# A linear-attention and MLP kernel: DMA transposes held back behind the third x chunk, natural x loads moved to the GpSimd queue

## The chip, the cores and the metric

The kernel runs on one core of a Trainium2 chip. A time is the device time of one execution in microseconds; lower is better. TensorE (PE) multiplies matrices, VectorE (DVE), ScalarE (ACT) and GpSimd (POOL) work on elements, and SyncE (SP) does little but issue DMAs. ACT and POOL can issue DMAs too. Every DMA runs on the core's 16 DMA engines.

## What is computed

One input x of 2048 rows by 640 columns in bf16 goes through two branches, which a gate per row mixes.

```python
g = _sigmoid((x * gate_w).sum(-1, keepdims=True))
# A: linear attention, 32 heads of 20 columns
q, k, v = split(x @ wqkv)
phi = lambda t: jnp.where(t > 0, t + 1, jnp.exp(t)) + 1e-6
kv  = einsum("bhsd,bhse->bhde", phi(k), v);  z = phi(k).sum(rows)
a   = (phi(q) @ kv / (phi(q) @ z + 1e-6)) @ wo
# B: token shift mixer, then an MLP of 1728 columns
h  = _gelu(_layernorm(x) @ w1)
x1 = x + shift(h) @ w2
b  = x1 + _gelu(_layernorm(x1) @ w3) @ w4
out = g * a + (1 - g) * b
```

(The block is shortened: `split`, `shift` and `phi(k).sum(rows)` stand for several lines each.)

## The kernel before

The 2048 rows are 16 chunks of 128. x is needed in SBUF in two forms. In the natural form, `x_sb` (a part of the buffer RXH), a chunk's rows lie on the partitions; in the turned form, `xT` (the buffer RXT), its columns do. TensorE contracts over partitions, so the products with the weights read `xT`, and the products that sum over rows (`g_step`, line 264) read `x_sb`.

Chunks 0 to 2 are loaded in natural form and turned by TensorE: `x_tr` (lines 317 to 323) makes five 128x128 transposes into two PSUM buffers, VectorE copies three of the results to `xT` (line 322) and ACT two (line 323). Chunks 3 to 15 are turned on the way in, by DMA transposes on the SP queue (`load_xT`, line 155), in nine pieces of one to three chunks, and are loaded in natural form a second time (`load_x`, line 152), in five pieces. `late_loads` (line 280) issues both kinds on SP in an alternating order, and behind them the weights wq, w1, wv, wo and w2. The first transpose is held back by a small trick: VectorE writes one column of chunk 3 of `xT` with a memset (line 328), and since the transpose overwrites that column it must wait for the memset. The other transposes stand behind it in SP's queue.

The instruction order on each engine is the order of the program (`manual_schedule`). DMAs share eight completion semaphores in turn, so each also waits for the DMA eight places earlier to have landed.

The first stage computes k = x @ wk for one chunk after another. `k_mm(c, p, dc)` (lines 253 to 256) is one pair of matmuls: row block dc of five of the weights, 512 and 130 columns, into PSUM buffer p. The weights arrive in four DMAs: row blocks 0, 1 and 2 on the ACT queue (line 162) and blocks 3 and 4 together on SP (line 169). For chunks 0 to 2 the pairs are taken in an order by hand (lines 325 to 343), so that TensorE has work while weights and chunks arrive. From chunk 3 on the loop at line 346 does five pairs per chunk, and after them `k_post` (ACT's exp at line 247, VectorE's lines 250 and 251, which read PSUM and release its buffer). From chunk 5 on the loop also interleaves `g_unit`, matmuls of line 264 on `x_sb` of chunks two or three places back. There are four PSUM buffers, passed round by `alloc` and `release`.

The second stage (line 388) computes q with wq, the later ones (lines 421 to 637) the mixer, the MLP and the gated sum. VectorE and ACT read `x_sb` for the layer norm (lines 218 and 229), chunk 3 first at the tenth chunk of the k stage.

Of the kernel before, what the change touches and what calls it, by code (L numbers as in the profile page):

```python
# [16 lines left out]
def kernel(  # L17
# [13 lines left out]
    nc = tc.nc  # L31
    P = 128
# [29 lines left out]
    xT = RXT[:].rearrange("p (j s) -> p j s", j=DC)  # L62
# [7 lines left out]
    x_sb = RXH[:, 0:NCH * D].rearrange("p (c d) -> p c d", c=NCH)  # L70
# [78 lines left out]
    xv = x2.rearrange("(c p) d -> p c d", p=P)  # L149

    def load_x(c0, c1):
        sp.dma_start(x_sb[:, c0:c1, :], xv[:, c0:c1, :])

    def load_xT(c0, c1):
        sp.dma_start_transpose(xT[:, :, c0 * P:c1 * P], x2[c0 * P:c1 * P, :])
# [97 lines left out]
    def k_mm(c, p, dc):  # L253
        for (n0, n1) in ((0, 512), (512, KW)):
            mm(PP[p][:, n0:n1], lhsT=xT[:, dc, c * P:(c + 1) * P], rhs=wkg[:, dc, n0:n1],  # L255
               start=(dc == 0), stop=(dc == DC - 1))
# [21 lines left out]
            g_post(i, gp[0])  # L278

    def late_loads():  # L280
        load_xT(3, 4)
        load_xT(4, 5)
        load_x(3, 4)
        load_xT(5, 6)
        load_xT(6, 7)
        load_x(4, 6)
        load_xT(7, 8)
        load_xT(8, 10)
        load_x(6, 9)
        load_xT(10, 11)  # L290
        load_xT(11, 13)
        load_x(9, 12)
        load_xT(13, 16)
        load_x(12, 16)
        rows = lambda w, a, b: w[:, a:b].rearrange("(j p) d -> p j d", p=P)
        sp.dma_start(wq, rows(A_wqkv, 0, D))
        sp.dma_start(w1, rows(B_w1, 0, D))
        sp.dma_start(wv, rows(A_wqkv, 2 * D, 3 * D))
        sp.dma_start(wo6[0:GW, 0:5, :], A_wo[0:5 * GW, :].rearrange("(g r) d -> r g d", r=GW))
        sp.dma_start(wo6[0:gsz[5], 5, :], A_wo[5 * GW:D, :])  # L300
        sp.dma_start(w2[:, 0:4, :], B_w2.rearrange("(g c) d -> c g d", c=CG)[0:P])
        for g in range(4):
            sp.dma_start(w2[32 * g:32 * (g + 1), 4, :], B_w2[CG * g + P:CG * (g + 1), :])
        w1g = w1.rearrange("p k (g c) -> p k g c", c=CG)
        w1x4 = w1x.rearrange("p k (g c) -> p k g c", g=4)
        for g in range(4):
            nc.gpsimd.tensor_copy(w1x4[:, :, g, :], w1g[:, :, g, P:CG])
# [9 lines left out]
    def x_tr(c, a, b):  # L317
        ta, tb = PP[a][:, 0:512].bitcast(BF16), PP[b][:, 0:512].bitcast(BF16)
        for dc in range(DC):
            t, k = (ta, dc) if dc < 3 else (tb, dc - 3)  # L320
            nc.tensor.transpose(t[:, k * P:(k + 1) * P], x_sb[:, c, dc * P:(dc + 1) * P], ident[:])
        nc.vector.tensor_copy(xT[:, 0:3, c * P:(c + 1) * P], ta[:, 0:3 * P].rearrange("p (j s) -> p j s", j=3))  # L322
        act(xT[:, 3:5, c * P:(c + 1) * P], tb[:, 0:2 * P].rearrange("p (j s) -> p j s", j=2), ACT.Copy)
# [1 line left out]
    for _ in range(3):  # L325
        alloc()
    x_tr(0, 3, 2)
    nc.vector.memset(xT[:, 0, 3 * P:3 * P + 1], 0.0)
    late_loads()
    x_tr(1, 1, 2)  # L330
    k_mm(0, 0, 0)
    k_mm(1, 1, 0)
    k_mm(0, 0, 1)
    k_mm(1, 1, 1)
    x_tr(2, 3, 2)
    k_mm(2, 2, 0)
    k_mm(2, 2, 1)
    for c in range(3):
# [348 lines left out]
```

## Time and profile before

| what | value |
|---|---|
| median of 3 runs | 266.31 us (266.26 to 266.87) |
| profiled execution | 267.08 us, of which the span from first to last instruction is 265.4 us |
| granted TensorE clock | 1.000 |
| DMA traffic | 23.95 MB in 42207 packets, 31052 of them under 512 B |
| issue time of a DMA transpose on SP | 1.2 to 2.8 us, median 1.27 us |
| landing of a DMA transpose | 3.0 to 5.2 us after issue, median 4.0 us |
| landing of a natural x load | 3.5 to 5.2 us after issue, median 4.7 us |

The page gives the busy time of each engine and its share of the span, then the span in 40 equal slices of 6.6 us with the busy share in tenths. The chain of waits is followed back from the last instruction, at each step to whatever released it. A timeline line has the start and the length in microseconds, engine, line, operation, destination and source, a count, and in brackets the idle time before it with what ended it. "SPq" means that the SP queue is issuing a DMA. A line of a DMA queue gives packets, megabytes and the time its packets took as a share of the 16 engines; packets in flight overlap, so this can pass 100%.

### The profile page before, as it was taken

To read this page: it belongs to the slowest core of one execution; us is meant where nothing else is said; L and a number is where in the kernel's file an instruction comes from. 1 tells how busy PE (TensorE), PEld (TensorE's weight loads), DVE (VectorE), ACT (ScalarE), POOL (GpSimd) and SP (SyncE) were. 2 spreads that over 40 slices of the span, in tenths; PEclk is the share of its full clock that TensorE was granted. 3 is DMA by queue.
4 is the path that set the end of the run, shared out by engine and by line. 5 is a ranking of instruction groups with operands and counts; after the bars stand their busy time and mean duration, and the time that the engine had idled before them with its cause. 6 is when DMAs were issued, how large, how long until landed. Compare 5 with 4: busy or idle time off the path is not lost.

```text
span 265.4 us, 4180 instructions
## 1 busy us (share of the span) xinstructions
PE 259.8 (98%) x1666; PEld 134.8 (51%) x1666; DVE 127.2 (48%) x227; ACT 109.7 (41%) x163; POOL 35.5 (13%) x118
## 2 busy tenths in 40 slices
PE   6999999999999999999999999999999999999995
PEld 2555555555564445554444455555544444555552
DVE  2386659888995257999920044233200002233242
ACT  3466654555454771334977512022034444022020
POOL 7000043030200000446870000000000000000000
PEclk9999999999999999999999999999999999999999
DMA  6899994452252069992542001001000000001001
GB/s 197 162 207 236 367 252 95 99 52 49 50 57 44 11 160 385 340 137 49 108 94 49 0 2 49 25 27 49 27 25 0 0 2 0 25 27 49 25 27 49
DMA packets 42207, 23.95 MB, mean 90 GB/s; under 512 B 31052, under 2 KB 41420, under 8 KB 42188
## 3 DMA queue, kind: packets, MB, share of 16 engines
q1 hardware_dynamic: 41602, 23.16, 36.4%
q10 hardware_dynamic: 586, 0.53, 0.6%
q8 instruction: 13, 0.21, 0.3%
q14 instruction: 6, 0.05, 0.1%
HBM read 12.86 MB, written 3.44 MB: 61 GB/s over the span
## 4 chain that ended last, share of the span: by engine, by line
PE 96%; DMA 2%; DVE 0%; ACTq 0%; ACT 0%; issue 0%
PE pp L637 20%; PE pp L570 20%; PE pp L421 8%; PE pp L596 8%; PE pp L555 8%; PE pp L264 8%; PE pp L255 8%; PE pp L388 8%; DMA RA<-in_A_wqkv_dram 2%; PE pp L579 2%; PE pp L622 1%; PE pp L631 1%; PE pp L586 1%; PE pp L455 1%; PE pp L441 1%; PE pp L468 0%
## 5 line engine op out<-in xcount | busy, mean ns | idle before, releaser
L637 PE MATMUL pp<-RB,RXH 128*128 128x512 bf16 (+1 forms) x390 | 54.4, 299 | 0.0
L570 PE MATMUL pp<-lnxT,RA 128*128 128x512 bf16 x240 | 52.1, 379 | 0.0
L637 PEld LDWEIGHTS <-RXH 128*128 128x128 bf16 x390 | 29.6, 98 | 24.2 <-issue 2.1
L570 PEld LDWEIGHTS <-RA 128*128 128x128 bf16 x240 | 23.4, 98 | 28.1
L599 ACT ACTIVATE RXH<-pp,g_all 128x640 f32<-128x640 f32 x16 | 12.7, 794 | 54.9 <-PE pp L596 54.9
L572 ACT ACTIVATE RXH<-pp 128x1024 bf16<-128x1024 f32 x24 | 24.3, 1020 | 26.7 <-PE pp L570 26.7
L247 ACT ACTIVATE eb<-pp 128x640 bf16<-128x640 f32 (+1 forms) x26 | 21.4, 828 | 25.0 <-PE pp L388 16.1
L264 PE MATMUL pp<-RPK,RXH 128*128 128x512 bf16 (+1 forms) x160 | 25.2, 299 | 0.0
L255 PE MATMUL pp<-RA,RXT 128*128 128x512 bf16 (+1 forms) x160 | 24.1, 299 | 1.0 <-DMA RA<-in_A_wqkv_dram 0.5
L601 DVE SCALAR_TENSOR_TENSOR RPK<-RPK,omg,RXH 128x640 f32<-128x640 f32 x8 | 7.1, 885 | 36.5 <-ACT RXH L599 36.5
L388 PE MATMUL pp<-RXT,RA 128*128 128x512 bf16 x100 | 23.2, 379 | 0.0
L596 PE MATMUL pp<-Mp,pqT 128*128 128x512 bf16 (+1 forms) x160 | 23.1, 299 | 0.0
L555 PE MATMUL pp<-w,RXH 128*128 128x512 bf16 (+1 forms) x160 | 21.9, 299 | 0.0
L601 DVE SCALAR_TENSOR_TENSOR RXT<-RXT,omg,RXH 128x640 f32<-128x640 f32 x8 | 7.1, 885 | 24.6 <-ACT RXH L599 24.6
L421 PE MATMUL pp<-lnxT,RB 128*128 128x512 bf16 x80 | 18.3, 380 | 0.0
L264 PEld LDWEIGHTS <-RXH 128*128 128x128 bf16 x160 | 12.7, 98 | 10.4
L255 PEld LDWEIGHTS <-RXT 128*128 128x128 bf16 x160 | 12.4, 98 | 10.8 <-DVE RXT L322 0.9
L596 PEld LDWEIGHTS <-pqT 128*128 128x128 bf16 x160 | 12.2, 98 | 10.0 <-issue 0.8
L555 PEld LDWEIGHTS <-RXH 128*128 128x128 bf16 x160 | 12.3, 98 | 9.6
L606 DVE SCALAR_TENSOR_TENSOR RXH<-pp,omg,RXT 128x640 bf16<-128x640 f32 x8 | 7.1, 884 | 19.8 <-PE pp L637 19.8
L606 DVE SCALAR_TENSOR_TENSOR RXH<-pp,omg,RPK 128x640 bf16<-128x640 f32 (+2 forms) x9 | 7.3, 810 | 19.1 <-PE pp L637 17.2
L388 PEld LDWEIGHTS <-RA 128*128 128x128 bf16 x100 | 11.1, 117 | 9.1
(107 smaller groups left out, 251.4 us busy)
## 6 DMA issues: line engine op xcount, KB each, us to landing
out_dram<-RXH SPq DMA_DIRECT2D x15, 160.0 KB, 1.8
RA<-in_B_w_dram SPq DMA_DIRECT2D x5, 432.0 KB, 6.7
RA<-in_A_wqkv_dram SPq DMA_DIRECT2D x2, 800.0 KB, 6.8
RB<-in_B_w_dram SPq DMA_DIRECT2D x1, 1120.0 KB
RXH<-in_A_x_dram SPq DMA_DIRECT2D x2, 480.0 KB, 5.1
RB<-in_B_w_dram SPq DMA_DIRECT2D x1, 960.0 KB, 12.2
RB<-in_B_w_dram SPq DMA_DIRECT2D x1, 800.0 KB, 8.5
Mp<-Mscr SPq DMA_DIRECT2D x1, 800.0 KB
```

Source lines behind the costliest of these rows:

```text
L247: act(e[:, 0:n], src, ACT.Exp)
L255: mm(PP[p][:, n0:n1], lhsT=xT[:, dc, c * P:(c + 1) * P], rhs=wkg[:, dc, n0:n1], start=(dc == 0), stop=(dc == DC - 1))
L264: mm(PP[p][:, n0:n1], lhsT=x_sb[:, c, i * P:(i + 1) * P], rhs=pk[:, c, n0:n1], start=(c == 0), stop=(c == NCH - 1))
L388: mm(PP[p][:, tt * 512:(tt + 1) * 512], lhsT=wqp[:, dc, j], rhs=xT[:, dc, t0:t0 + 512], start=(dc == 0), stop=(dc == DC - 1))
L421: mm(PP[p][:, tt * 512:(tt + 1) * 512], lhsT=lh, rhs=lnxT[:, dc, t0:t0 + 512], start=(dc == 0), stop=(dc == DC - 1))
L555: mm(PP[p][:, n0:n1], lhsT=hsT[:, fc, 2 + c * P:2 + (c + 1) * P], rhs=w2[:, fc, n0:n1], start=(fc == 0), stop=(fc == DC - 1))
L570: mm(PP[p][:, k * 512:(k + 1) * 512], lhsT=w3[:, dc, (fc + k) * P:(fc + k + 1) * P], rhs=lnxT[:, dc, t * 512:(t + 1) * 512], start=(dc == ...
L572: act(h2T[:, t % 2, fc:fc + 2, :], PP[p][:].rearrange("p (k s) -> p k s", k=2), ACT.Gelu_apprx_tanh)
L596: mm(PP[p][:, n0:n1], lhsT=pqT[:, j, c * P:(c + 1) * P], rhs=Mp[:, j, n0:n1], start=(j == 0), stop=(j == DC - 1))
L601: nc.vector.scalar_tensor_tensor(x1(c), x1(c), omg[:, c:c + 1], ga, op0=ALU.mult, op1=ALU.add)
L606: nc.vector.scalar_tensor_tensor(oc[:, n0:n1], PP[p][:, n0:n1], omg[:, c:c + 1], x1(c)[:, n0:n1], op0=ALU.mult, op1=ALU.add)
L637: mm(PP[p][:, n0:n1], lhsT=h2T[:, k, fc, cc], rhs=w4[:, fc, n0:n1], start=False, stop=(fc == NF - 1))
```

## The change

In `late_loads` all nine transposes now come first on the SP queue, and the five natural loads are issued by GpSimd. The call of `late_loads` moves behind `x_tr(2, 3, 2)`, and `x_tr(2, 3, 2)` itself moves up, ahead of the pairs of weight row block 1. The memset that holds the transposes stands behind the copies of chunk 2, and a second memset, on one column of chunk 3 of `x_sb`, holds the natural loads in the same way.

```diff
     def late_loads():
-        load_xT(3, 4)
-        load_xT(4, 5)
-        load_x(3, 4)
-        load_xT(5, 6)
-        load_xT(6, 7)
-        load_x(4, 6)
-        load_xT(7, 8)
-        load_xT(8, 10)
-        load_x(6, 9)
-        load_xT(10, 11)
-        load_xT(11, 13)
-        load_x(9, 12)
-        load_xT(13, 16)
-        load_x(12, 16)
+        for (c0, c1) in ((3, 4), (4, 5), (5, 6), (6, 7), (7, 8), (8, 10), (10, 11), (11, 13), (13, 16)):
+            load_xT(c0, c1)
+        for (c0, c1) in ((3, 4), (4, 6), (6, 9), (9, 12), (12, 16)):
+            nc.gpsimd.dma_start(x_sb[:, c0:c1, :], xv[:, c0:c1, :])
         rows = lambda w, a, b: w[:, a:b].rearrange("(j p) d -> p j d", p=P)
...
     x_tr(0, 3, 2)
-    nc.vector.memset(xT[:, 0, 3 * P:3 * P + 1], 0.0)
-    late_loads()
     x_tr(1, 1, 2)
     k_mm(0, 0, 0)
     k_mm(1, 1, 0)
+    x_tr(2, 3, 2)
+    nc.vector.memset(xT[:, 0, 3 * P:3 * P + 1], 0.0)
+    nc.vector.memset(x_sb[:, 3, 0:1], 0.0)
+    late_loads()
     k_mm(0, 0, 1)
     k_mm(1, 1, 1)
-    x_tr(2, 3, 2)
     k_mm(2, 2, 0)
```

## What was predicted

> **What bounds the kernel now.** I read first the page's engine line and slices, then the chain of waits over the first 20 us, then the timelines of TensorE and of the SP queue, then the DMA view cut to windows. TensorE holds the span:
>
> ```profile
> PE 259.8 (98%) x1666; PEld 134.8 (51%) x1666; DVE 127.2 (48%) x227; ACT 109.7 (41%) x163; POOL 35.5 (13%) x118
> PE   6999999999999999999999999999999999999995
> DMA  6899994452252069992542001001000000001001
> PE 96%; DMA 2%; DVE 0%; ACTq 0%; ACT 0%; issue 0%
> ```
>
> TensorE is idle for 5.6 of 265.4 us, and only in the first and the last slices. The DMA row beside it is full in the first slices: while chunks of x arrive the 16 engines are busy. The chain and the timeline say where the early idle time lies:
>
> ```profile
> 1.79 4.86 DMA RA<-in_A_wqkv_dram
> 7.40 0.29 PE pp L321 x5
> 7.71 0.39 ACT RXT L323
> 8.15 7.25 PE pp L255 x52
> ...
> 5.23 0.91 PE L255 MATMUL pp<-RA,RXT 128*128 128x512 bf16 x4
> 6.69 0.70 PE L255 MATMUL pp<-RA,RXT 128*128 128x512 bf16 x4 [0.55 <-DMA RA<-in_A_wqkv_dram]
> 7.23 0.44 PE L321 MATMUL pp<-ident,RXH 128*128 128x128 bf16 x5
> 8.15 7.25 PE L255 MATMUL pp<-RA,RXT 128*128 128x512 bf16 x52 [0.47 <-ACT RXT L323]
> ```
>
> TensorE waits 0.55 us for the second row block of the K weights (landed 6.65), turns x chunk 2 from 7.23, and waits 0.47 us for the copies of it. From 8.15 on it never stops until the last outputs, so a microsecond won or lost before 8.15, and any new wait after it, reaches the end one for one. The SP queue in this stretch issues without a pause:
>
> ```profile
> 4.97 2.60 SPq L155 DMA_TRANSPOSE RXT<-in_A_x_dram  x2
> 7.62 0.58 SPq L152 DMA_DIRECT2D RXH<-in_A_x_dram  x1
> 8.24 2.53 SPq L155 DMA_TRANSPOSE RXT<-in_A_x_dram  x2
> 10.82 0.58 SPq L152 DMA_DIRECT2D RXH<-in_A_x_dram  x1
> 11.44 2.58 SPq L155 DMA_TRANSPOSE RXT<-in_A_x_dram  x2
> ```
>
> A transpose of one chunk takes SP about 1.27 us. Those issued at 8.24 and 9.46 landed after 3.4 and 3.0 us. The natural loads stand between the transposes in the same queue: that order throttles them.
>
> **What the Trainium skill says.** "DMA: Bandwidth & Descriptors", section "Issuing engines are not separate DMA queues": DMAs of SP, ACT and GpSimd run on the same 16 engines and interleave; issuing from more engines saves issue time alone. Section "Queues, rings and completion order": an engine goes round its queues packet by packet. The trace agrees for two queues of equal packets; from 3 to 6 us SP's and ACT's loads moved almost equal numbers:
>
> ```profile
> q1 hardware_dynamic: 425, 0.50, 54.3%
> q10 hardware_dynamic: 388, 0.45, 41.5%
> ```
>
> It shows no transpose beside a load of another queue. In "SWDGE vs HWDGE vs iDMA" the page says that GpSimd DMAs have their descriptors written by software, with the first byte after about 1 us; no run here shows it yet. "SBUF — State Buffer" (the "DVE blocks DMA" trap) adds that this writing and VectorE's 2-port modes exclude each other; the trace of before has no such DMA.
>
> **The change, part by part.**
>
> Order of TensorE. The 5 transposes of chunk 2 move from after k_mm(1, 1, 1) to before k_mm(0, 0, 1). Chunk 2 of x is issued at 1.7 and lands after 4.7 us (the longest of the L152 landings there), so at 6.4. TensorE turns it at 6.45 to 6.9 instead of standing still for 0.55 us. The four matmuls of row block 1 (0.54 us, 6.69 to 7.23) follow to 7.45; VectorE's copy (0.36 after a 0.37 us lag, 7.18) and ACT's (0.38 us) are done by then, so the 0.47 us wait goes. What stood at 8.15 begins at about 7.49. Gain 0.66 us. Next late would be weight rows 3 and 4 (issued 2.18, landing 5.6, so 7.8), needed only after five more pairs of 0.273 us, at 8.9: hidden.
>
> The hold. The first transpose waits for a VectorE memset that now follows the copy of chunk 2: copy at 6.82, memset at about 7.2, issue at 7.25 instead of 4.97, 2.3 us later. Queued behind it on SP are all nine transposes and then the weights wq, w1, wv, wo, w2; on VectorE nothing waits behind 0.06 us memsets (its next work is the exp of chunk 0 near 10). The weights lose nothing: taking five loads out of the queue gives back 4 x 0.58 + 1.5 = 3.8 us of SP. What the hold buys I put at zero, between 0 and 0.3: the transposes' small packets begin only near 6.2 by the traffic rate, when the weight block that TensorE waited for had all but arrived.
>
> Transposes alone. With a cadence of 1.27 us and 3.2 us to landing, chunks 3 to 7 land at 10.45, 11.7, 13.0, 14.3, 15.5. TensorE wanted them at 11.15 (8.15 plus 11 pairs of 0.273), 12.5, 13.9, 15.94, 17.98 by the chain; less 0.66 that is 10.5, 11.85, 13.2, 15.3, 17.3. All are in time, the first three by 0.05 to 0.2 us. The margin of over 2 us that chunk 3 had is spent.
>
> Natural loads on POOL. Five DMAs, 13 chunks, start behind the second memset at about 7.3 with POOL idle until 33, so the first bytes move at about 8.3 (skill's 1 us), the rest about one DMA per us. Nobody needs them soon: chunk 3 is first read by L264 at 17.4. But now nothing throttles them. Prices from windows where one kind runs alone (23.2 to 24.8 us transposes, 26 to 31 us loads):
>
> ```profile
> q1 hardware_dynamic: 1685, 0.43, 127.3%
> ...
> q1 hardware_dynamic: 1492, 1.87, 106.1%
> ```
>
> A 256 B packet costs 1.273 x 16 x 1.6 / 1685 = 19 ns of an engine, a 1,280 B row 1.061 x 16 x 5 / 1492 = 57 ns. A transposed chunk is 640 small packets, 40 an engine, 0.77 us; a natural chunk is 8 rows an engine, 0.455 us, all 13 together 5.9 us. Transposes use 0.77 of each 1.27 us, so 0.5 us per slot is free. The question is how an engine shares:
> - transposes favoured (they go as several small packets against one row): no stall, 0 to 0.3 us;
> - in order of arrival: before chunk 5 stand 6 natural chunks, 2.73 us, less three free slots of 0.5: 1.2 us late, 14.2 against 13.2; before chunk 7 all 13, 5.9 less 2.5: 3.4 us late, 18.9 against 17.3. Stall 1.6 us;
> - one row for each small packet: chunk 3 meets 8 rows, chunks 4 and 5 forty each, 88 x 57 ns = 5.0 us less 1.5: chunk 5 lands at 16.5 against 13.2. Stall 3.3 us.
> The sharing seen above (near equal packets) speaks for the last, the GpSimd's slower supply for the second. I take the middle, 2.5 us. The stall falls in TensorE, with no slack behind.
>
> Sum: -0.66 + 2.5 = +1.8 us on the profiled run, 267.08 us (span 265.4 and 1.7 around it); that run lies 0.77 us above the median of 266.31, and the difference carries over: 268.1 us.
>
> **Rivals.**
> - Forecast: the natural loads crowd the transposes; 267.3 (arrival order) to 269.0 (one for one). For it: DMA slices at 0.8 to 1.0 while both are being loaded. Against: rows and small packets never met across queues in this trace.
> - Not slower: transposes keep their pace, and the reorder's 0.66 us remains less 0 to 0.3: 265.65 to 266.0. It decides as long as a transposed chunk needs no more than about 1.3 us in the engines, that is if fewer than 9 rows (0.5 us) get ahead of its 40 packets. For it: such packets may be handed over in larger groups. This is a no-change by measurement.
> - Lock: descriptor writing on POOL and VectorE's L250 (324 ns, bf16) hold each other up near 10 to 13 us. VectorE frees PSUM for TensorE with little to spare (L251 of chunk 0 ends at 12.28, chunk 4 starts at 12.5), so a block of about 1 us costs 0.8: 266.4 to 267.4, with the transposes otherwise in time. POOL may be done by then, which speaks against it.
> - More gained than I count: weight block 1 and chunk 2 land some 0.3 us sooner without small packets about, 265.3. Against it: they overlap by a few tenths at most.
>
> **How the numbers follow.** Forecast 0.50, transposes keep pace 0.33, lock 0.10, larger gain 0.07. About 0.3%, 0.8 us, is what a measurement of this kernel can tell from no change. Slower by more: 0.46 of the forecast case and 0.08 of the others, 0.54. Faster by more needs under 265.5: the larger gain and a sliver of the second case, 0.12. The rest, 0.34, is within. The range 265.6 to 269.2 takes the second case at its favourable end and the one-for-one sharing at the other; the forecast's own is 267.2 to 269.1.
>
> **What would show it.** Right: L321 in one run of ten to fifteen before the second weight block, no 0.47 us wait on L323, the first transpose at about 7.25, then TensorE waiting for DMA RXT<-in_A_x_dram around chunks 4 to 7, 1.6 to 3.3 us in all, while a GpSimd queue fills the DMA row. Wrong: no such wait and transposes landing in 3 us as before; or waits on VectorE for PSUM instead; or transposes with long landings whose chunks TensorE still has.

## The result and the profile after

| kernel | median of its runs | range | ratio to before (95% interval) |
|---|---|---|---|
| before | 266.36 us (6 runs) | 266.26 to 266.87 | |
| changed | 277.97 us (6 runs) | 275.74 to 278.50 | 1.0421 [1.0384, 1.0459] |

The change costs 11.6 us where 1.8 were forecast, and the time lies above the range, which ended at 269.2. The profiled execution took 278.5 us, with a span of 276.8, so the span grew by 11.4 us. Here and in the table of experiments a ratio leaves out runs more than 1.5% above the fastest of the same kernel, which now and then occur whatever the kernel; e2_pool keeps one run of four that way and has no ratio.

The page of the changed kernel: busy time by engine, then the slices (6.9 us each), then the two queues that issue most DMAs.

```profile
PE 261.1 (94%) x1634; PEld 136.2 (49%) x1666; DVE 127.6 (46%) x228; ACT 109.8 (40%) x163; POOL 39.2 (14%) x123
PE   7725999999999999999999999999999999999995
PEclk9995999999999999999999999999999999999999
DMA  5799995145043205999254100010010000001001
q1 hardware_dynamic: 39858, 21.03, 32.6%
q0 software_dynamic: 496, 2.13, 3.4%
```

Two things are new. TensorE's row has a hole in the third slice (13.8 to 20.8 us), and the granted clock has a dent in the fourth, right behind it. From the fifth slice on both rows are as before: the whole loss lies before 28 us. The second queue, q0, is GpSimd's: 2.13 MB in 496 packets. 416 of these carry the data, which is 5,120 B or four rows of x each, where the queues of SP and ACT move one row of 1,280 B a packet.

The timeline of the changed kernel from 4 to 30 us (start, length, engine, what, and in brackets the idle time before it):

```profile
6.99 3.84 PE L255 MATMUL pp<-RA,RXT 128*128 128x512 bf16 x25
7.43 21.99 SPq L155 DMA_TRANSPOSE RXT<-in_A_x_dram  x9
7.74 3.82 POOL L284 DMA_DIRECT2D RXH<-in_A_x_dram  x5 [1.43 <-DVE RXH L323]
11.07 1.52 PE L255 MATMUL pp<-RA,RXT 128*128 128x512 bf16 x10 [0.25 <-DVE eb L250]
14.57 1.54 PE L255 MATMUL pp<-RA,RXT 128*128 128x512 bf16 x10 [1.98 <-DVE eb L250]
23.62 2.86 PE L255 MATMUL pp<-RA,RXT 128*128 128x512 bf16 x10 [7.51 <-DMA RXT<-in_A_x_dram]
26.27 1.27 PE L264 MATMUL pp<-RPK,RXH 128*128 128x512 bf16 x4
```

The groups of ten are chunks 3, 4 and 5. Before them TensorE stands for 0.25, 1.98 and 7.51 us, 9.74 in all. The first two waits are put down to VectorE's L250, but these matmuls do not read `eb`: the transpose of chunk 3 landed at 10.93, and that of chunk 4, issued at 8.77, landed 5.8 us later, at 14.53. The transposes issued at 10.08 and 11.4 landed after 13.5 and 12.8 us; before the change the slowest of this stretch took 4.0. SP issued one after the other with gaps of 0.05 us, so none of them stood waiting for one of the shared semaphores. The chain of waits of the changed kernel says it in three pieces (start, length, what):

```profile
8.77 1.26 SPq L155
10.03 0.04 issue
10.08 13.50 DMA RXT<-in_A_x_dram
...
23.62 2.86 PE pp L255 x10
26.48 1.07 PE pp L264 x4
```

Chunk 5 then takes 2.86 us instead of about 1.4, and the four L264 matmuls 1.07 instead of 0.54. The view by windows shows why (window, length, busy time and count of PE, PEld, DVE, ACT and POOL, granted clock, DMA share, GB/s):

```profile
14.00:16.00 2.00, 1.43 (x10) 0.73 (x10) 1.36 (x3) 0.00 (x0) 0.00 (x0) 1.00 1.04 314
16.00:20.00 4.00, 0.11 (x2) 0.00 (x0) 1.15 (x2) 1.48 (x4) 0.00 (x0) 1.00 1.28 115
20.00:25.00 5.00, 1.38 (x5) 0.65 (x6) 0.00 (x0) 0.00 (x0) 0.00 (x0) 0.58 1.05 183
25.00:30.00 5.00, 4.95 (x28) 2.66 (x28) 1.39 (x3) 1.74 (x5) 0.00 (x0) 0.74 1.15 157
...
21.00:27.50 6.50, 3.88 (x15) 1.93 (x16) 0.25 (x1) 0.77 (x2) 0.00 (x0) 0.50 1.29 183
```

After the long idle the clock is granted at half: 0.50 from 21 to 27.5 us (0.58 and 0.74 are means over windows that hold some time at full rate). The Trainium skill, "TensorE: Matmul & The Clock Gate", section "Why this matters for your kernels", says that an idle gap of more than about 3 us drops TensorE to half rate. The trace agrees: the gap of 1.98 us left the clock at 1.00, the one of 7.51 us did not (the 2.44 us wait of e10_held_paced, below, puts the bound lower). The same rows show the DMA engines counted as full throughout, but from 14 to 16 us they deliver 314 GB/s, and after that only 115 and 183.

The sum: idle 9.7 us, chunk 5 slow by 1.5, L264 by 0.5, less 0.4 us that TensorE was ahead before chunk 3 (its earlier pairs end at 10.83 here; the same 11 pairs, 22 matmuls, counted from 8.15 in the kernel before end at 11.2). That is 11.3 of the 11.4 us by which the span grew.

### The profile page after: what moved, and what is told of

Its sections match the earlier page's. It is cut to its first block, busy times and chain, and to the rows that moved or that the text cites. A ratio compares the mean times of both kernels' runs of the same rounds, so it can differ in the third digit from the quotient of the medians.

```text
span 276.8 us, 4156 instructions
## 1 busy us (share of the span) xinstructions
PE 261.1 (94%) x1634; PEld 136.2 (49%) x1666; DVE 127.6 (46%) x228; ACT 109.8 (40%) x163; POOL 39.2 (14%) x123
## 3 DMA queue, kind: packets, MB, share of 16 engines
q0 software_dynamic: 496, 2.13, 3.4%
## 4 chain that ended last, share of the span: by engine, by line
PE 91%; DMA 5%; SPq 1%; issue 1%; DVE 1%; ACT 0%
PE pp L628 19%; PE pp L561 19%; PE pp L264 8%; PE pp L412 8%; PE pp L587 8%; PE pp L546 8%; PE pp L379 8%; PE pp L255 6%; DMA RXT<-in_A_x_dram 5%; PE pp L570 2%; PE pp L613 1%; PE pp L622 1%; PE pp L301 1%; SPq L155 1%; PE pp L577 1%
## 5 line engine op out<-in xcount | busy, mean ns | idle before, releaser
L628 PE MATMUL pp<-RB,RXH 128*128 128x128 bf16 (+1 forms) x382 | 53.9, 298 | 0.4
L561 PEld LDWEIGHTS <-RA 128*128 128x128 bf16 x240 | 23.4, 98 | 28.0
L247 ACT ACTIVATE eb<-pp 128x640 bf16<-128x640 f32 (+1 forms) x26 | 21.4, 828 | 37.0 <-PE pp L255 20.8
L255 PE MATMUL pp<-RA,RXT 128*128 128x130 bf16 (+1 forms) x156 | 26.2, 314 | 9.9 <-DMA RXT<-in_A_x_dram 7.5
L264 PE MATMUL pp<-RPK,RXH 128*128 128x512 bf16 (+1 forms) x158 | 25.6, 302 | 0.1
L255 PEld LDWEIGHTS <-RXT 128*128 128x128 bf16 x160 | 13.1, 103 | 20.6 <-DMA RXT<-in_A_x_dram 10.2
L546 PE MATMUL pp<-w,RXH 128*128 128x128 bf16 (+1 forms) x157 | 21.7, 297 | 0.2
L250 DVE TENSOR_SCALAR eb<-eb 128x640 bf16<-128x640 bf16 (+1 forms) x26 | 9.6, 371 | 22.8 <-ACT eb L247 22.8
L264 PEld LDWEIGHTS <-RXH 128*128 128x128 bf16 x160 | 12.9, 99 | 10.8 <-issue 0.6
```

The costliest lines, as they stand in the source:

```text
L247: act(e[:, 0:n], src, ACT.Exp)
L264: mm(PP[p][:, n0:n1], lhsT=x_sb[:, c, i * P:(i + 1) * P], rhs=pk[:, c, n0:n1], start=(c == 0), stop=(c == NCH - 1))
L546: mm(PP[p][:, n0:n1], lhsT=hsT[:, fc, 2 + c * P:2 + (c + 1) * P], rhs=w2[:, fc, n0:n1], start=(fc == 0), stop=(fc == DC - 1))
L561: mm(PP[p][:, k * 512:(k + 1) * 512], lhsT=w3[:, dc, (fc + k) * P:(fc + k + 1) * P], rhs=lnxT[:, dc, t * 512:(t + 1) * 512], start=(dc == ...
L628: mm(PP[p][:, n0:n1], lhsT=h2T[:, k, fc, cc], rhs=w4[:, fc, n0:n1], start=False, stop=(fc == NF - 1))
```

## The experiments

All were compared with the kernel before on the same chip, whose medians lay between 266.5 and 266.9 us.

| run | what is different | median, us | ratio (95% interval) |
|---|---|---|---|
| e1_hold | changed, loads all on SP in the old order | 267.61 | 1.0031 [1.0007, 1.0055] |
| e2_pool | before, natural loads on GpSimd | 276.81 | none |
| e3_reorder | before, chunk 2 turned earlier | 266.40 | 0.9991 [0.9975, 1.0007] |
| e4_act | changed, ACT in GpSimd's place | 276.30 | 1.0345 [1.0310, 1.0381] |
| e5_pool2 | before, 3 chunks on GpSimd | 266.74 | 1.0004 [0.9982, 1.0026] |
| e6_act2 | before, the same 3 on ACT | 267.05 | 1.0009 [0.9994, 1.0024] |
| e7_serial | changed, transposes after the loads | 278.52 | 1.0451 [1.0428, 1.0475] |
| e8_half | changed, loads in half columns | 273.82 | 1.0296 [1.0255, 1.0337] |
| e9_paced | before, 13 chunks on GpSimd, paced | 266.95 | 1.0017 [0.9997, 1.0037] |
| e10_held_paced | changed, paced | 270.76 | 1.0143 [1.0107, 1.0179] |
| e11_pool6 | before, 6 chunks on GpSimd at once | 273.12 | 1.0210 [1.0163, 1.0257] |
| e12_early_paced | e9_paced, chunk 2 turned earlier | 266.18 | 0.9998 [0.9985, 1.0012] |
| e13_act6 | before, 6 chunks on ACT, a little later | 269.33 | 1.0110 [1.0054, 1.0166] |
| e14_pool6 | the same on GpSimd | 268.43 | 1.0050 [0.9992, 1.0108] |
| e15_extra_act | before, 0.88 MB extra on ACT | 268.26 | 1.0046 [1.0021, 1.0070] |
| e16_extra_pool | the same on GpSimd | 267.76 | 1.0043 [1.0028, 1.0058] |
| e17_other_src | changed, natural loads from B_x | 277.15 | 1.0387 [1.0337, 1.0438] |
| e18_plain256 | changed, plain loads for transposes | 268.94 | 1.0089 [1.0056, 1.0122] |

### Which part of the change costs the time

e1_hold keeps the hold and the early turning of chunk 2 and puts the old list of `late_loads` back, all on SP:

```diff
-        for (c0, c1) in ((3, 4), (4, 5), (5, 6), (6, 7), (7, 8), (8, 10), (10, 11), (11, 13), (13, 16)):
-            load_xT(c0, c1)
-        for (c0, c1) in ((3, 4), (4, 6), (6, 9), (9, 12), (12, 16)):
-            nc.gpsimd.dma_start(x_sb[:, c0:c1, :], xv[:, c0:c1, :])
+        load_xT(3, 4)
+        load_xT(4, 5)
+        load_x(3, 4)
...
```

> Only the hold and the earlier turning of chunk 2; all loads stay on the SP queue in the alternating order of the kernel before. Theory A (a second queue of natural loads beside the transposes makes them crawl, whichever engine issues it) and theory B (only loads issued by GpSimd do, for their 5,120 B packets): 265.8 us, between 265.4 and 266.4, every transpose landing within 4 us. Theory C (holding the transposes for 2.3 us is what makes them late): 268 us or more, with TensorE waiting for transposes of chunks 3 to 5.

Measured: 267.61 us, between what the theories said. The hold spends the margin, and with it comes a wait. Timeline of e1_hold:

```profile
6.15 6.52 PE L255 MATMUL pp<-RA,RXT 128*128 128x512 bf16 x45
13.85 1.54 PE L255 MATMUL pp<-RA,RXT 128*128 128x512 bf16 x10 [1.18 <-DMA RXT<-in_A_x_dram]
18.48 1.54 PE L255 MATMUL pp<-RA,RXT 128*128 128x512 bf16 x9 [0.64 <-DMA RXT<-in_A_x_dram]
```

The transposes of chunks 5 to 9 landed after 3.3 to 5.3 us (3.0 to 4.0 before), but the first was issued 1.7 us later (6.65 in place of 4.97), and TensorE stood 1.8 us. Hold and early turn together cost about 0.8 us (0.3%), a fraction of the loss.

e2_pool is the other part alone: nothing held, chunk 2 at its old place, natural loads on GpSimd.

```diff
     def late_loads():
-        load_xT(3, 4)
-        load_xT(4, 5)
-        load_x(3, 4)
-        ...
+        for (c0, c1) in ((3, 4), (4, 5), (5, 6), (6, 7), (7, 8), (8, 10), (10, 11), (11, 13), (13, 16)):
+            load_xT(c0, c1)
+        for (c0, c1) in ((3, 4), (4, 6), (6, 9), (9, 12), (12, 16)):
+            nc.gpsimd.dma_start(x_sb[:, c0:c1, :], xv[:, c0:c1, :])
...
     nc.vector.memset(xT[:, 0, 3 * P:3 * P + 1], 0.0)
+    nc.vector.memset(x_sb[:, 3, 0:1], 0.0)
     late_loads()
```

> Only the natural loads on GpSimd; nothing is held, chunk 2 is turned where it was. A and B: the transposes that meet the natural loads crawl as in the changed kernel, one of chunks 4 to 6 landing over 8 us after its issue; 272 to 278 us. C: 266.3 us, as before.

Measured: 276.81 us (270.43 to 279.37 in four runs); all four lie above the 268.91 us of the slowest of 33 runs of the kernel before, but the spread is wide, so the size of the loss is not settled by this run. In the profile, which is of the slowest run, the transposes issued at 7.6 and 8.9 us landed after 13.4 and 17.7 us, and TensorE waited 7.13 and 2.21 us for them. The long landings come with GpSimd's loads, held or not.

e3_reorder moves only `x_tr(2, 3, 2)` ahead of the second pair of weights:

```diff
     k_mm(1, 1, 0)
+    x_tr(2, 3, 2)
     k_mm(0, 0, 1)
     k_mm(1, 1, 1)
-    x_tr(2, 3, 2)
```

> Only the transposes of chunk 2 on TensorE ahead of weight block 1; transposes start at about 5 us as before. All theories: 265.7 us (between 265.4 and 266.1), the 0.47 us wait on ACT's copy of chunk 2 gone. If the change gains nothing here either, the gain I counted at 0.66 us is not there.

Measured: 0.9991 [0.9975, 1.0007], nothing that can be told. In its profile TensorE waited 0.89 us for chunk 2 of x, which landed at 6.9, in place of 0.55 us for the weights. Turning chunk 2 earlier exchanges one wait for another, and which is longer depends on whichever transfer happens to land last.

### GpSimd, or any second queue? And how much?

e4_act is the changed kernel with the five loads on ACT's queue:

```diff
+        for (c0, c1) in ((3, 4), (4, 6), (6, 9), (9, 12), (12, 16)):
+            aq.dma_start(x_sb[:, c0:c1, :], xv[:, c0:c1, :])
...
-        for (c0, c1) in ((3, 4), (4, 6), (6, 9), (9, 12), (12, 16)):
-            nc.gpsimd.dma_start(x_sb[:, c0:c1, :], xv[:, c0:c1, :])
```

> The changed kernel with the natural loads issued by ACT instead of GpSimd, so a second queue with packets of one 1,280 B row. A: transposes crawl as with GpSimd or worse, 274 to 285 us. B: transposes land within 5 us, TensorE waits at most 2 us for them, 265.7 to 268.5 us.

Measured: 276.30 us, but for another reason. Timeline of e4_act, and under it what held ACT up (engine, line, what it waited for, us):

```profile
6.68 9.96 ACTq L282 DMA_DIRECT2D RXH<-in_A_x_dram  x5
11.75 1.52 PE L255 MATMUL pp<-RA,RXT 128*128 128x512 bf16 x10 [1.81 <-DMA RXT<-in_A_x_dram]
18.77 4.31 PE L255 MATMUL pp<-RA,RXT 128*128 128x512 bf16 x20 [5.50 <-DVE RPK L251]
...
ACT eb L247 <- DMA RXT<-in_A_x_dram: 10.0, 1, 10.0
```

From its first issue to its last ACT took 9.96 us, where GpSimd took 3.82 for the same five DMAs. An issue alone takes ACT 0.33 to 0.50 us. The rest is waiting for completion semaphores: the fourth load was issued at 9.31, when ACT's own first had landed (9.29), and the fifth at 16.26, when the transpose of chunk 5 had landed (16.24). SP and ACT take turns with the same eight semaphores; in the changed kernel each of GpSimd's five loads has one of its own and waits for none. So ACT's exp came late, PSUM stayed occupied and TensorE waited for VectorE. The transposes landed after 4.8 to 6.9 us, 6.9 for chunk 5. Its landing at 16.2 is close to the 16.5 us of the prediction's one-for-one sharing, but does not show that sharing: from 6.7 to 16.3 us 2894 small packets went through beside 1152 rows. The total time says nothing about the queue here.

The next runs vary the amount, at first three chunks on either queue:

```diff
     def late_loads():
+        for (c0, c1) in ((3, 4), (4, 6)):
+            nc.gpsimd.dma_start(x_sb[:, c0:c1, :], xv[:, c0:c1, :])
         load_xT(3, 4)
         load_xT(4, 5)
-        load_x(3, 4)
...
-        load_x(4, 6)
```

> Order and start of the transposes as before; only the first two natural loads (chunks 3 to 5, 6 of the 26 packets an engine gets from GpSimd in the changed kernel) go to GpSimd, the other three stay between the transposes on SP. Theory B (loads issued by GpSimd slow the transposes beyond their own traffic): chunk 4 or 5 lands over 5 us after its issue, 267.5 to 270.5 us. Theory A (any second queue, one packet for one, nothing beyond the traffic): chunk 5 at most 2 us late, which its margin covers, 266.0 to 267.0 us.

> The same two loads on ACT's queue instead of GpSimd's, everything else as in e5_pool2. A: like e5_pool2 within 0.5 us. B: no transpose lands later than 5 us after its issue and the time stays at 266.0 to 267.2 us, while e5_pool2 is slower.

Measured: 1.0004 and 1.0009, both no change; transposes landed after 3.8 to 5.7 and 3.9 to 5.8 us. Three chunks do no harm that can be told, whoever issues them. e11_pool6 adds (6, 9) to the list on GpSimd.

> As e5_pool2, with a third load on GpSimd at once (chunks 3 to 8, 12 of 26 packets an engine). E: the backlog is twice that of e5_pool2 and falls on chunks 5 to 7, whose margin is 2 us; one of them lands 5 to 9 us after issue, 266.5 to 271 us, between e5_pool2 and the kernel with all five. If the crawl needs the largest loads only: as e5_pool2, 266.0 to 267.0 us.

Measured: 273.12 us. The transpose issued at 7.6 landed after 10.8 us, those behind it after 9.9, 9.2 and 9.1, and TensorE stood 5.15 us and then ran chunk 5 in 2.85. With 0, 3, 6 and 13 chunks handed to GpSimd at once the times are 266.5, 266.7, 273.1 and, in the changed kernel, 278.0 (276.8 in e2_pool): issued this early, the harm begins between three and six.

### Are the loads slow by themselves, or do both kinds disturb each other?

e7_serial lets no transpose run beside the loads: GpSimd copies a column of the last natural chunk into `xT`, which the first transpose must wait for.

```diff
         for (c0, c1) in ((3, 4), (4, 6), (6, 9), (9, 12), (12, 16)):
             nc.gpsimd.dma_start(x_sb[:, c0:c1, :], xv[:, c0:c1, :])
+        nc.gpsimd.tensor_copy(xT[:, 0, 3 * P:3 * P + 1], x_sb[:, 15, 0:1])
+        for (c0, c1) in ((3, 4), (4, 5), (5, 6), (6, 7), (7, 8), (8, 10), (10, 11), (11, 13), (13, 16)):
+            load_xT(c0, c1)
```

> The changed kernel with the first transpose held until the last natural load of GpSimd has landed, so the two kinds never meet. B: alone, the loads need about 7 us (landed by 15), the transposes then land at 1.3 us intervals from 18 on; TensorE waits once, about 7 us, and warms up again: 272 to 276 us, less than the changed kernel although everything that TensorE needs starts 8 us later. Rival D (GpSimd's loads are slow by themselves, with or without transposes beside them): the loads end at 20 or later, and the time is 280 us or more.

Measured: 278.52 us, later than expected. Timeline of e7_serial:

```profile
7.72 3.83 POOL L282 DMA_DIRECT2D RXH<-in_A_x_dram  x5 [1.41 <-DVE RXH L324]
17.66 0.18 POOL L283 COPY RXT<-RXH 128x1 bf16<-128x1 bf16 x1 [6.11 <-DMA RXH<-in_A_x_dram]
17.87 13.12 SPq L155 DMA_TRANSPOSE RXT<-in_A_x_dram  x9
20.89 5.93 PE L255 MATMUL pp<-RA,RXT 128*128 128x512 bf16 x30 [10.04 <-DMA RXT<-in_A_x_dram]
```

Alone, the loads landed 2.6 to 6.8 us after issue (beside the transposes 3.0 to 12.8) and all were there before 17.7. Then the transposes took 2.9 us each, at a cadence of 1.3, which puts chunk 5 at 23.4. In the changed kernel it landed at 23.57. So running both kinds together brought chunk 5 no sooner than running them one after the other. The DMA view over one and the same window, 7.4 to 23.6 us, shows what the overlap was worth (queue: packets, MB, share of 16 engines). The changed kernel:

```profile
q0 software_dynamic: 496, 2.13, 58.9%
q1 hardware_dynamic: 2907, 0.71, 38.9%
```

and e7_serial:

```profile
q0 software_dynamic: 496, 2.13, 40.9%
q1 hardware_dynamic: 2189, 0.54, 15.5%
```

The window is 16.2 us, or 259 us of 16 engines. The same 2.13 MB took 0.589 x 16.2 = 9.5 us of each engine beside transposes and 6.6 us alone. A small packet took 0.389 x 259 / 2907 = 35 ns beside loads and 18 ns alone, which is the 19 ns of the prediction. The mixture takes 98% of the window for what would cost 58% at the prices of either kind alone (2907 x 19 ns and 1664 rows x 57 ns are 150 of 259 us). These are times in flight, which overlap (the windows of the prediction's prices reach 106 and 127%), so they are no measure of a limit; the landings above show the loss without them.

The 35 ns are an average that hides how the loss comes about. Of the 2907 small packets (256 B, and some of 4 B), 2641 took 22 ns or less, as they do alone; 192 took over 100 ns, up to 819, and about half of the time is theirs. GpSimd's packets have a median of 225 ns, with single ones up to 3361. More than half of these long packets fall between 16 and 22 us, where the traffic drops to 125 GB/s, from 216 between 7.4 and 16.

e8_half cuts each load in two halves of the columns. Of its 576 data packets 416 are of 4,480 B (seven pieces of 640 B), the rest smaller; the changed kernel's are of 5,120.

```diff
-            nc.gpsimd.dma_start(x_sb[:, c0:c1, :], xv[:, c0:c1, :])
+            for (h0, h1) in ((0, D // 2), (D // 2, D)):
+                nc.gpsimd.dma_start(x_sb[:, c0:c1, h0:h1], xv[:, c0:c1, h0:h1])
```

> The changed kernel with each natural load cut into two of half the columns, rows of 640 B. If GpSimd's packets are four rows (5,120 B in the changed kernel), they become 2,560 B and twice as many. If the cost goes with the number of changes between the two kinds on an engine: slower than the changed kernel, 280 us or more. If it goes with the size of the packet that each small one waits for: faster, 270 to 276 us.

Measured: 273.82 us, with waits of 0.96, 0.25, 1.47, 1.40 and 2.08 us spread over the chunks and none long enough for the clock. But GpSimd also needed 7.26 us to issue ten DMAs where it needed 3.82 for five, so the loads arrived more slowly: the run loses less than the changed kernel, and does not tell packet size from pace.

### Pace

e9_paced hands GpSimd three chunks at once and the other ten one at a time, each held by a memset on VectorE behind a `k_post`; nothing else is held.

```diff
+    def pool_x(c):
+        if 6 <= c < NCH:
+            nc.vector.memset(x_sb[:, c, 0:1], 0.0)
+            nc.gpsimd.dma_start(x_sb[:, c, :], xv[:, c, :])
...
+            for (c0, c1) in ((3, 4), (4, 6)):
+                nc.gpsimd.dma_start(x_sb[:, c0:c1, :], xv[:, c0:c1, :])
...
         k_post(c, p)
+        pool_x(c + 5)
```

(Four GpSimd copies that wait for w1 also move behind the loop, since they would stand ahead of the loads.)

> All 13 natural chunks on GpSimd as in the changed kernel, nothing held, chunk 2 turned where it was; but only chunks 3 to 5 at once, chunks 6 to 15 one at a time, each behind a memset after the k stage's element work of five chunks earlier. Theory E (it is the backlog that GpSimd's queue builds up beside the transposes, not the queue or the bytes): transposes land within 5 us, no wait of TensorE for them, 266.0 to 267.0 us. Theory B (GpSimd's loads slow transposes whatever their pace): 270 us or more.

Measured: 266.95 us, 1.0017 [0.9997, 1.0037]. All 13 chunks go through GpSimd's queue and the loss is gone: the transposes landed after 3.9 to 7.4 us, where 5 had been expected, but TensorE never waited for one. e10_held_paced is the changed kernel with the same pacing.

> The changed kernel itself, with hold and early turning of chunk 2, but its natural loads paced as in e9_paced. E: the hold alone is left, at most 1 us of waits for chunks 3 to 5 against about 0.4 us gained at the start: 265.9 to 267.2 us. B: 270 us or more.

Measured: 270.76 us, above what was expected. Timeline of e10_held_paced:

```profile
10.17 1.52 PE L255 MATMUL pp<-RA,RXT 128*128 128x512 bf16 x10 [0.38 <-DMA RXT<-in_A_x_dram]
12.34 2.90 PE L255 MATMUL pp<-RA,RXT 128*128 128x512 bf16 x20 [0.65 <-DMA RXT<-in_A_x_dram]
21.77 2.86 PE L255 MATMUL pp<-RA,RXT 128*128 128x512 bf16 x10 [2.44 <-DMA RXT<-in_A_x_dram]
```

Later transposes landed after up to 9.4 us, somewhat more than in e9_paced, and the hold has used up the margin that covered the delay there. The chunk after the 2.44 us wait again takes 2.86 us, and the clock from 21.4 to 24.7 us is granted at 0.50. e12_early_paced is e9_paced with chunk 2 turned earlier, as in e3_reorder, and no hold.

> e9_paced with chunk 2 turned early and the transposes not held: the version that should keep the gain at the start and nothing else. E: 265.7 to 266.5 us, at best 0.5 us under the kernel before, which these rounds may not tell from no change. B: 270 us or more.

Measured: 266.18 us over 22 runs, 0.9998 [0.9985, 1.0012]. Its profile still shows one wait of 0.89 us for a late transpose. No version beat the kernel before by an amount that can be told.

### The twins: queue and packet size

e13_act6 and e14_pool6 differ in one word of the program. The transposes of chunks 3 and 4 go out as before; three loads (six chunks) go to the second queue behind the turning of chunk 2.

```diff
     x_tr(2, 3, 2)
+    nc.vector.memset(x_sb[:, 3, 0:1], 0.0)
+    for (c0, c1) in ((3, 4), (4, 6), (6, 9)):
+        aq.dma_start(x_sb[:, c0:c1, :], xv[:, c0:c1, :])
+    late_loads()
```

> x chunks 3 to 8 in natural form issued at once (three DMAs) on ACT's queue behind x_tr(2) at its old place, the rest of late_loads on SP, nothing held, chunk 2 turned at its old place. The same six chunks on GpSimd in e11_pool6 gave 273.1 us and transposes that landed 9 to 11 us after issue. Theory G (it is the issue by GpSimd as such, with its large packets or without): transposes land at most 6.5 us after issue, TensorE waits for RXT under 1 us in all, 266.0 to 268.5 us. Theory Q (any second queue with so much waiting data does it): transposes land 8 us or more after issue, 269 to 274 us. ACT's own standing at the issue may hold its exp and copies; that is read apart, by the landings.

> The twin of e13_act6, line for line, with GpSimd issuing the three loads in place of ACT. Both theories: transposes issued beside the loads land 8 us or more after issue, TensorE waits 3 us or more for RXT, 269 to 274 us. If this one keeps its transposes under 6.5 us, then the place of the issue decided in e11_pool6 and not the amount.

Measured: 1.0110 [1.0054, 1.0166] on ACT and 1.0050 [0.9992, 1.0108] on GpSimd; the intervals overlap, and neither expectation was met. Transposes landed after 5.9 to 7.2 us beside ACT's loads and 2.9 to 8.9 beside GpSimd's, with medians of 6.4 and 6.6. In the profiles TensorE waited 1.0 us for transposes on GpSimd and none on ACT, where weights that landed late (1.1 us) had set it back anyway. So a second queue delays the transposes whoever issues it. The DMA view from 8 to 16 us of e13_act6,

```profile
q1 hardware_dynamic: 2878, 0.70, 51.0%
q10 hardware_dynamic: 686, 0.83, 50.0%
```

and of e14_pool6:

```profile
q0 software_dynamic: 206, 0.87, 56.5%
q1 hardware_dynamic: 1915, 0.47, 35.5%
```

For equal load data (0.83 and 0.87 MB) 2878 small packets went through beside ACT's loads and 1915 beside GpSimd's, one profile each. The twins are not quite alike in time: ACT's second and third loads waited for landed transposes, by the shared semaphores, and the third was issued at 10.58, GpSimd's at 9.74. Both mixtures are dear: at the prices of either kind alone (19 and 57 ns) ACT's is worth 94 of the 129 us that it took and GpSimd's 75 of 118, factors of 1.4 and 1.6, where the changed kernel's 150 of 253 are 1.7. That e11_pool6, with the same six chunks on GpSimd 1.8 us earlier, lost 2% shows how near the edge this amount lies.

e15_extra_act and e16_extra_pool keep every load of the kernel before and add two loads with rows of 3,456 B behind the turning of chunk 2.

```diff
+    nc.vector.memset(lnxT[:, 0, 0:1], 0.0)
+    for dc in range(2):
+        aq.dma_start(lnxT[:, dc, 0:F], B_w3[dc * P:(dc + 1) * P, :])
```

> The loads of the kernel before, in its order on SP, and behind x_tr(2) two extra loads on ACT's queue of 128 rows of 3,456 B each (0.88 MB in all) that move data nobody uses into a buffer that is free then. It is about as much data as six x chunks (0.98 MB), with rows 2.7 times as long. Theory F (large packets hold the transposes up, whoever issued them): transposes beside them land 7 us or more after issue and the time is 269 us or more. Theory G (the issue by GpSimd as such): transposes land at most 6.5 us after issue, 266.0 to 268.5 us.

> The twin of e15_extra_act with the two extra loads (data nobody uses) on GpSimd. Theories F and G both: transposes beside them land 7 us or more after issue, 269 us or more. If the transposes of this one land under 6.5 us, the delay belongs to many rows of x on GpSimd and not to GpSimd's loads in general.

Measured: 1.0046 and 1.0043, transposes landing after 2.8 to 5.4 and 4.7 to 6.2 us, and no wait for one in either profile; where their 0.4% come from is not shown. Neither long rows nor GpSimd as the issuer is enough by itself. In these two the transposes stay spaced by plain loads in SP's own queue, which the six-chunk twins lack.

### Where the data come from, and what kind of small packet

e17_other_src changes only the source of GpSimd's loads:

```diff
-            nc.gpsimd.dma_start(x_sb[:, c0:c1, :], xv[:, c0:c1, :])
+            nc.gpsimd.dma_start(x_sb[:, c0:c1, :], xbv[:, c0:c1, :])
```

> The changed kernel, with GpSimd's five natural loads reading the same rows of B_x, an input of the same shape that the reference never uses, in place of A_x; x in natural form is therefore not x for chunks 3 to 15. Number, size and order of all DMAs stay. Theory S (transposes and natural loads delay each other because both read the same tensor in DRAM): transposes land at most 7 us after issue, TensorE waits under 2 us for RXT, 266.5 to 270 us. Theory Q (13 chunks waiting on GpSimd's queue at once hold the transposes up, wherever they come from): chunk 5 lands 12 us or more after issue, 275 to 279 us, as the changed kernel (277.97).

Measured: 277.15 us, and chunk 5 landed 11.7 us after issue, a hair under the 12 expected. Up to that landing, at 21.3, its small packets took 28 ns on average, so the loss does not hang on one fixed price. That both kinds read one tensor is not the cause.

e18_plain256 replaces the transposes by plain loads of the same 256 B pieces:

```diff
-        sp.dma_start_transpose(xT[:, :, c0 * P:c1 * P], x2[c0 * P:c1 * P, :])
+        for c in range(c0, c1):
+            sp.dma_start(xT[:, :, c * P:(c + 1) * P], x2[c * P:(c + 1) * P, :].rearrange("p (j s) -> p j s", j=DC))
```

> The changed kernel with each DMA transpose replaced by plain loads on SP, one per chunk (13 in place of nine), that put the same 128 rows into the same place of xT in pieces of 256 B, not turned; k, q and all that follows from them are therefore not of x for chunks 3 to 15. GpSimd's 13 natural chunks stay as they are. Theory T (DMA transposes alone are held up by GpSimd's loads): the plain loads that run beside them land at most 7 us after issue and TensorE waits under 2 us for RXT, 266 to 269 us. Theory M (any DMA of many small packets is held up by the large ones waiting): chunk 5 lands 9 us or more after issue, TensorE waits over 4 us, 271 us or more.

Measured: 268.94 us, 1.0089 [1.0056, 1.0122]. The piece of chunk 5 landed after 6.7 us and TensorE waited 2.5 us for such loads in two places, a little over the 2 of theory T; its DMA view from 7.4 to 23.6 us:

```profile
q1 hardware_dynamic: 6647, 1.67, 50.3%
q0 software_dynamic: 496, 2.13, 38.8%
```

The same 2.13 MB of GpSimd take 6.3 us of each engine, as they do alone, and a small packet takes 0.503 x 259 / 6647 = 20 ns, none of the 256 B ones over 56. No price rises, and 6647 small packets go through where the transposes managed 2907. Plain loads wait their turn (up to 10.0 us, for chunk 7), but nothing is wasted. Among the kinds tried, the rise belongs to transposes that run beside the loads. SP issues plain loads every 0.68 us in place of 1.3, so this run is not a pure exchange of kind.

**What stays open.** Why single packets stand for up to 3 us when transposes and rows mix was not seen in any view; nor whether GpSimd's four-row packets are the reason that its loads hold the transposes up more than ACT's, if they do. A run with one-row packets on GpSimd was not tried.

## Why the prediction was wrong

**What bounds the kernel.** Right. Any wait after the start of the K products reached the end one for one: 11.3 us of waits and slow matmuls explain 11.4 us of span.

**Order of TensorE, minus 0.66.** The mechanics came out as written: the run after the turning of chunk 2 started at 6.99, the 0.47 us wait went, the pairs end 0.4 us earlier. Of this only 0.1 us was kept, since chunk 3 landed at 10.93, just late. e3_reorder shows that the gain is not dependable.

**The hold at zero.** Wrong by about 0.8 us (the ratio of e1_hold; 0.2 to 1.5 by its interval). The issue at 7.25 was right (7.44), as was "the margin is spent". What failed was to go on with landings of 3.2 us for every transpose, when the spread seen before reached 4.0 in this stretch. With a margin of 0.05 to 0.2 us that spread is a stall: e1_hold measured 1.18 and 0.64 us.

**Natural loads on POOL, plus 2.5.** This is the step that failed, and it carries nearly the whole error: a stall of 2.5 us was forecast, and TensorE stood 9.74. The step priced the loads at 57 ns a row and the transposes at 19 ns a packet, from windows in which one kind ran alone, and then laid out three ways of sharing, of which the worst cost 3.3 us. Against the 13.2 at which TensorE wanted chunk 5, three parts make up the 23.6 at which it landed:
- Up to 16.5 the worst sharing of the prediction reaches. Its choice of 2.5 us in the middle was too low already.
- The order adds little. Chunk 5, third in the transposes' queue, landed with GpSimd's last load (issued 10.8, landed after 12.8 us), so nearly everything issued until then was done before it: 13 natural chunks and 2907 small packets (4.5 chunks). At the clean prices these are 5.9 + 3.5 = 9.4 us of each engine, from 7.7 to 17.1.
- The rest is some 6 us. About 1 of it is the start, since no packet of either kind moved before 8.8, and about 5 are the price of the mixture: in flight both kinds took 9.5 + 6.3 = 15.8 us of each engine in place of 9.4. e7_serial and e18_plain256 show that neither the loads alone nor the loads beside plain pieces cost so much.

A hint of the price stood in the trace of before. In its window from 14 to 24 us transposes and rows ran mixed on SP's queue, and 4490 small packets and 768 larger ones took 110.9% of the 16 engines, 177 us, where the clean prices give 129: a factor of 1.37. The long packets stood there too (up to 1505 ns). With this factor the 9.4 us become 12.9, chunk 5 lands at 20.6, and the range would have held a stall of 7 us.

The Trainium skill, "DMA: Bandwidth & Descriptors", section "Issuing engines are not separate DMA queues", says that the DMAs of all engines interleave on the same 16. The traces agree: ACT's loads delayed SP's transposes to landings of up to 6.9 us in e4_act and 7.2 in e13_act6. But the section says nothing of the shares. The equal shares that the prediction read from SP and ACT between 3 and 6 us were those of equal packets, and were no measure for four-row packets beside transposes. The first byte of a GpSimd DMA after about 1 us, which the prediction took from that page, stands there under "Specifications"; here the first packet moved 1.9 us after the issue began, and 1.5 in e7_serial.

**The clock.** Not priced at all. A stall of 7.5 us costs 2.0 us more afterwards. With a stall of 7 us in the bounds this would have belonged to them.

**The rivals.** "Transposes keep pace" is out. A hold between POOL and VectorE shows, but is small: the one L250 that ran while GpSimd was still issuing took 445 ns, and the later ones 317 to 326, as before the change. In e8_half, where GpSimd issued for longer, three took 500 to 612. The waits of TensorE named after L250 were for transposes. Of what was to be seen, the early turn, the issue near 7.25, the missing 0.47 us wait and waits for RXT around chunks 4 and 5 came; their sum was 9.7 us in place of 1.6 to 3.3.

## What to carry to other kernels

A queue that is full of transfers nobody needs yet is not free because it is on an idle engine. Its order among the others, one behind the other on SP, was what kept the urgent transposes short; before taking that throttle away, work out the case in which all of the moved data goes first, and put it into the range. If a second queue is wanted, hand it its loads piece by piece: 13 chunks at once cost 11.6 us, paced, with nothing held, they cost nothing that can be told (with the hold 4.3 us, e10_held_paced). Price a mixture of transfers from a window in which it is mixed, and add the slow clock to any TensorE stall of several microseconds.

## What the runs showed that was not expected

Plain loads in 256 B pieces beside GpSimd's loads cost 20 ns a packet, DMA transposes beside the same loads 35 on average, because about one in fifteen stood for 0.1 to 0.8 us. ACT needed 9.96 us for the five loads that GpSimd issued in 3.82, because its fourth and fifth waited for semaphores that it shares with SP; GpSimd's loads have semaphores of their own. So moving a load to another engine also changes which landing it has to wait for. And a wait of 2.44 us in e10_held_paced was already followed by a chunk of 2.86 us, while 1.98 us in the changed kernel and 2.08 us in e8_half were not, so 3 us is no safe bound for the clock here.
